# Keeping both parts of every expert unit for the second half of outputs, running the second products one pair later, and decoding weights down to six free slots

## The chip, the core and the metric

The kernel runs on one core of a Trainium2 chip. The metric is the device time of one execution in microseconds, taken over several timed runs; lower is better. The kernel is one program of some 6,600 instructions on five engines: TensorE (PE: matmuls, PEld: loads of the stationary operand), VectorE (DVE), ScalarE (ACT), GpSimd (POOL) and SyncE (SP, which issues every DMA).

## The reference

Two batches of 12 attention heads (448 positions, head size 64) with a tanh cap on the scores, then two feed-forward layers on the 896 x 768 result. Cut to what matters:

```python
scores = cap * np.tanh(q @ k.T / 8 / cap)
attn = softmax(scores);  x = attn @ v                       # (896, 768)
h = x @ w_in                                                # (896, 2048)
P = a[0] + a[1]*h + a[2]*h*h + a[3]*h*h*h
Q = 1.0 + abs(b[0])*abs(h) + abs(b[1])*h*h
g = P / (Q + 1e-6)
x2 = g @ w_out                                              # (896, 768)
y = maximum(maximum(x2 @ w1, x2 @ w2), x2 @ w3)             # (896, 768)
out = y @ w_out2
```

The weights of both layers arrive as 64-bit floats. The result is 32-bit.

## The kernel before, in words

**Numbers.** A matmul operand is held in two parts, a rounded high part and the remainder (`hi`, `lo`), and a product is three matmuls: hi x hi, hi x lo, lo x hi (`three`, line 419). So x, g, x2 and each weight tile exist as pairs of tiles.

**Stages.** Attention comes first: for each of 12 pairs of heads, `prep` loads q, k, v and makes the parts; `scores` (lines 508 to 551) runs the score matmuls (line 520), tanh (L532) and exp (L535); `weighted` (line 553) multiplies with v (L576); the result is copied out of PSUM (`xu`, L588), its row sums travel through DRAM (`sums`, `comp`, `rsum`, `row`), and the scaled result is split into `x{batch}_{pair}` (L630 to L639). Next the first feed-forward layer, in 32 units of 128 hidden channels x 448 tokens, two units to a pair k = 0 to 15. `up` (line 648) makes h of a unit with 18 matmuls (L661). ACT and DVE turn h into g: `A` (L678), `W` (L681, L692, L695), `T` (L685, L687, L700), and for a whole pair `rational` (L716 to L726). `parts` (line 735) splits g of the pair into `gh` (L740) and `gl` (L743). `down` (line 752) multiplies the parts with the weights of the first half of outputs (`oa`) or of the second half (`ob`), nine matmuls a unit (L769). After both halves come the three branches (L851) and the last product (L910).

**Order of the first layer** (lines 797 to 828). Units are made `LAG` = 2 pairs ahead: for each k the program has the parts of k, `up` of pair k+2, then `down("oa")` of pair k. The second half of outputs follows: first the last `KEEP` = 4 pairs, whose parts are still there, then pairs 0 to 11, for which `parts` is called a second time (line 823).

**Weights.** `weight` (line 360) loads a tile in 64 bits into one of three raw buffers and decodes it in six steps: scale (L369 on ACT or L371 on POOL), shift (L375, DVE), rest (L394 on DVE or L391 on ACT), sign (L384, DVE), the high part (L411) and the low part (L399, DVE or POOL).

**What sets the order.** All steps are handed to a planner (`Flow`, line 65) with a cost on each engine that may do them, and it lays them out in time before the program is written; each engine then runs its instructions in exactly that order. A step is due when the PE step that needs it starts; ready steps are taken in order of their due times. SBUF is cut into 52 slots (`NSLOT`); a step that wants a new slot early, more than 14 of the planner's microseconds before it is due, must leave `LEAVE` = 9 of them free (line 123). PSUM is four tiles b0 to b3 of two banks each. In the first layer's first half six banks hold sums (three output blocks x two batches) and two hold the h of the units in work. Waits between engines come with the recorded order: the row lists show that a matmul into one bank of a tile waits for earlier reads of the other bank of that tile.

Of the kernel before, what the change touches and what calls it, by code (L numbers as in the profile page):

```python
# [25 lines left out]
NFC = DFF // P  # L26
# [3 lines left out]
QGUARD = 1.0 + 1e-6  # L30
CAP = 6
NG = 4
LAG = 2
NSLOT, NRAW, NROW = 52, 3, 3
WARM = 4

SPLIT = ()

KEEP = 4

AHEAD, NEAR, LEAVE = 120.0, 24.0, 9

SHARE = 0.5

# [224 lines left out]
def attention_moe(ctx: ExitStack, tc: tile.TileContext, qk, v, w_in, w_out, w123, w_out2, par, out):  # L269
    nc = tc.nc  # L270
    dve, act, pool, pe = nc.vector, nc.scalar, nc.gpsimd, nc.tensor
# [88 lines left out]
    def weight(key, src):  # L360
# [44 lines left out]
        fetched[0] = got  # L405
        s1 = add({"act": 0.80, "pool": 0.87}, scale, [got], [raw, dec], leave=LEAVE, ahead=AHEAD)
        s2 = add({"dve": 0.47}, shift, [s1], [dec], shared=True)
        s3 = add({"dve": 0.87, "act": 0.98}, rest, [s2], [raw, dec], shared=True)
        s4 = add({"dve": 0.87}, sign, [s3], [raw, dec], shared=True)
        s5 = add(  # L410
            {"act": 0.74, "dve": 0.47}, lambda e: copy_on[e](flat(hi), flat(dec)), [s4], [dec, hi],  # L411
# [12 lines left out]
    units += [(fc, b) for fc in range(NG, NFC) for b in range(B)]  # L424
    NU = len(units)
    NK = NU // 2
    again = list(range(NK - KEEP, NK)) + list(range(NK - KEEP))
    for n in range(NG):
        weight(("in", n), w_in[n])
        if n % 2:  # L430
# [1 line left out]
    for j in range(NG // 2, NFC // 2):  # L432
        weight(("in", 2 * j), w_in[2 * j])
        weight(("in", 2 * j + 1), w_in[2 * j + 1])
        weight(("oa", j), w_out[0, j])
    for k in again:
        for fc in dict.fromkeys(units[2 * k + i][0] // 2 for i in range(2)):
            if ("ob", fc) not in weights:
                weight(("ob", fc), w_out[1, fc])
    for oc in range(NCC):  # L440
        for m in range(3):
            weight(("m", oc, m), w123[oc, m])
# [65 lines left out]
    def scores(pi, half):  # L508
# [12 lines left out]

        for t in ts:
            t.early = pi < B * NPAIR - 3
        done = add({"pe": 1.25}, products, prepared, [uq, uk, *ts])
        for th in last_tanh[-2:]:
            th.before(done)
        for j in range(2):
# [25 lines left out]
    def weighted(i):  # L553
# [5 lines left out]
        for half in range(2):  # L559
            x, ex, h = E.pop((i, half))  # L560

            def products(e, half=half, x=x, h=h):
                dst, t = bank(o)[:, :S], two(x)[:CP]
                terms = []
                if h is None:
                    w = flat(vr).rearrange("p (c b d) -> p c (b d)", c=NCH, b=3)
                    for n in range(2):
                        terms.append((w[:CP, 2 * half + n, j * D : j * D + 2 * D], t[:, n]))
                else:
                    w = flat(vs).rearrange("p (t c b d) -> p t c (b d)", t=2, c=2, b=3)  # L570
                    for n in range(2):
                        hi, lo = (w[:CP, z, n, j * D : j * D + 2 * D] for z in range(2))
                        th, tl = two(h)[:CP, n], t[:, n]
                        terms += [(hi, th), (lo, th), (hi, tl)]
                for m, (w_, t_) in enumerate(terms):
                    pe.matmul(dst, w_, t_, start=half == 0 and m == 0, stop=half == 1 and m == len(terms) - 1)  # L576

            dep = add(
                {"pe": 1.66 if h is None else 1.2}, products, [ex, got_v, vl, dep],
                [o, x, vr] + ([h, vs] if h is not None else []),  # L580
            )
            if half == 0 and len(last_copy) > 1:
                last_copy[-2].before(dep)
# [151 lines left out]
    def parts(k):  # L735
        g, dep = G[k]
        hi, lo = slot(f"gh{k}", F32R), slot(f"gl{k}", F32R)

        def high(e):
            copy_on[e](two(hi), two(g))  # L740

        def low(e):
            engine[e].tensor_tensor(out=two(lo), in0=two(g), in1=f32(two(hi)), op=ALU.subtract)  # L743

        h_ = add({"act": 0.845, "dve": 0.54}, high, [dep], [g, hi], shared=True)
        l_ = add({"dve": 1.0, "pool": 2.1}, low, [h_], [g, hi, lo], shared=True)
        GH[k], GL[k] = (hi, h_), (lo, l_)
        G[k] = g, l_

    acc, count = {}, {}  # L750

# [66 lines left out]
    for b in range(B):  # L818
        for o in range(3):
            finish_x2(b, o)  # L820
    for k in again:
        if k < NK - KEEP:
            parts(k)
        down("ob", 2 * k, 1)
        down("ob", 2 * k + 1, 1)
    for b in range(B):
# [152 lines left out]
```

## Time and profile before

| | us |
|---|---|
| median of 3 runs (567.91 to 569.79) | 568.99 |
| the profiled execution | 566.61 |
| its span, first to last instruction | 564.8 |
| PE busy | 536.9 (95%) |
| DVE busy | 402.0 (71%) |
| ACT busy | 318.3 (56%) |
| POOL busy | 58.5 (10%) |

The profile was taken on one execution; the span is the time from its first to its last instruction, and 1.8 us of the execution's time lie around it. Busy shares are means over stages with different limits, so the stages are read one by one. PE's matmuls overlap each other in the records (a matmul of 448 columns is shown with about 365 ns, while the next starts some 200 ns later), so a busy PE is not a proof that nothing holds it, but an idle PE is time lost.

### The profile page before, as it was taken

Reading aid. Unit: us, or ns where it says so; the run is one execution under the profiler, and the core shown is the slowest. Engines: PE = TensorE matmul, PEld = TensorE weight load, DVE = VectorE, ACT = ScalarE, POOL = GpSimd, SP = SyncE. Lnnn points to the kernel's source line nnn. Section 1 sums busy time; section 2 is a strip of 40 time slices with the busy share of each in tenths; the row PEclk is TensorE's granted clock in tenths of the full one; section 3 lists DMA queues with packets and bytes.
Section 4 is the critical chain, followed back from the end, with each engine's and each line's share of the span. In section 5 each row is a group of like instructions: output and inputs, shape, how many; then the busy total and the mean of one; then the engine's idle time right before and its main releaser. Section 6 shows DMA issues by size and latency. Waiting matters only on the chain.

```text
span 564.8 us, 6604 instructions
## 1 busy us (share of the span) xinstructions
PE 536.9 (95%) x2544; PEld 445.2 (79%) x2544; DVE 402.0 (71%) x556; ACT 318.3 (56%) x397; POOL 58.5 (10%) x49
## 2 busy tenths in 40 slices
PE   8999999979978998999899799999999999999997
PEld 5555555548867887887788689999999999999997
DVE  5688999487879999988799989779997473121000
ACT  5899999875567686657776763125443252011111
POOL 0201001100111123010001131210010000000000
PEclk9999999999999999999999899999999999999999
DMA  8666847134000122000132256454455110000112
GB/s 273 220 218 206 274 141 241 63 102 146 18 1 1 56 89 79 2 0 14 43 113 82 86 169 224 167 174 161 169 182 208 57 57 1 1 1 0 57 58 82
DMA packets 17168, 59.79 MB, mean 106 GB/s; under 512 B 3736, under 2 KB 7064, under 8 KB 17136
## 3 DMA queue, kind: packets, MB, share of 16 engines
q1 hardware_dynamic: 17136, 59.36, 30.6%
q8 instruction: 20, 0.33, 0.2%
q14 instruction: 12, 0.10, 0.1%
HBM read 56.47 MB, written 2.88 MB: 105 GB/s over the span
## 4 chain that ended last, share of the span: by engine, by line
PE 66%; DVE 17%; ACT 11%; issue 3%; DMA 3%; SPq 0%; ACTq 0%; DVEq 0%
PE b L851 23%; PE b L769 15%; PE b L661 10%; PE b L910 8%; PE b L576 6%; PE b L520 4%; DMA qk<-in_qk_dram 3%; ACT raw L391 3%; DVE W L723 2%; ACT e L532 2%; DVE W L692 2%; DVE gl L743 2%; DVE W L695 2%; ACT e L535 2%; DVE T L720 2%
## 5 line engine op out<-in xcount | busy, mean ns | idle before, releaser
L851 PE MATMUL b<-x,whm 128*128 128x448 f32 x432 | 122.6, 365 | 0.0
L661 PE MATMUL b<-x,whin 128*128 128x448 f32 x384 | 111.5, 372 | 1.6 <-DVE W L692 1.2
L851 PEld LDWEIGHTS b<-x,whm 128*128 128x128 f32 x432 | 81.1, 188 | 6.4
L576 PE MATMUL b<-e,vr 112*128 112x448 f32 x192 | 80.0, 556 | 2.2 <-issue 2.1
L661 PEld LDWEIGHTS b<-x,whin 128*128 128x128 f32 x384 | 71.8, 188 | 11.3 <-DVE W L692 1.9
L851 PE MATMUL b<-x,wlm 128*128 128x448 f32 x216 | 78.9, 365 | 0.0
L661 PE MATMUL b<-x,wlin 128*128 128x448 f32 x192 | 70.2, 366 | 0.0
L576 PEld LDWEIGHTS b<-e,vr 112*128 112x128 f32 x192 | 34.8, 191 | 36.1 <-issue 31.5
L769 PE MATMUL b<-gh,whoa 128*128 128x448 f32 x96 | 37.3, 389 | 15.6 <-DVE W L692 7.9
L535 ACT ACTIVATE e<-e,con 112x896 f32<-112x896 f32 x48 | 47.9, 1064 | 0.0
L391 ACT ACTIVATE raw<-raw 128x768 uint8<-128x768 uint8 x24 | 46.7, 1956 | 0.1
L532 ACT ACTIVATE e<-b 112x896 f32<-112x896 f32 x48 | 42.3, 944 | 6.9 <-PE b L520 6.9
L851 PEld LDWEIGHTS b<-x,wlm 128*128 128x128 f32 x216 | 40.6, 188 | 3.2
L520 PEld LDWEIGHTS b<-uq,uk 64*112 64x112 f32 x288 | 25.5, 181 | 20.4 <-issue 7.2
L520 PE MATMUL b<-uq,uk 64*112 64x448 f32 x288 | 39.2, 397 | 1.1 <-ACT e L532 1.0
L661 PEld LDWEIGHTS b<-x,wlin 128*128 128x128 f32 x192 | 36.1, 188 | 2.9
L769 PE MATMUL b<-gl,whoa 128*128 128x448 f32 x96 | 36.0, 375 | 2.2 <-DVE gl L743 2.2
L769 PEld LDWEIGHTS b<-gh,whoa 128*128 128x128 f32 x96 | 18.4, 192 | 22.9 <-DVE W L692 10.9
L411 ACT CAST whm<-decm 128x768 fp32r<-128x768 f32 x15 | 12.6, 837 | 42.0 <-DVE decm L384 42.0
L879 ACT CAST h3h<-t 128x448 fp32r<-128x448 f32 x10 | 5.7, 568 | 53.9 <-DVE t L874 53.9
L769 PE MATMUL b<-gh,wloa 128*128 128x448 f32 x96 | 35.7, 372 | 0.0
L769 PE MATMUL b<-gh,whob 128*128 128x448 f32 x96 | 35.2, 366 | 0.3 <-ACT x L785 0.3
(110 smaller groups left out, 976.2 us busy)
## 6 DMA issues: line engine op xcount, KB each, us to landing
raw<-in_w_out_dram SPq DMA_DIRECT2D x22, 768.0 KB, 4.3
raw<-in_w_dram SPq DMA_DIRECT2D x18, 768.0 KB, 4.1
raw<-in_w_in_dram SPq DMA_DIRECT2D x16, 768.0 KB, 5.8
qk<-in_qk_dram SPq DMA_DIRECT2D x12, 448.0 KB, 6.3
vr<-in_v_dram SPq DMA_DIRECT2D x12, 336.0 KB, 4.4
row<-rsum SPq DMA_DIRECT2D x24, 112.0 KB, 3.0
out_dram<-ob SPq DMA_DIRECT2D x6, 384.0 KB, 2.7
out_dram<-ob SPq DMA_DIRECT2D x2, 192.0 KB, 1.9
```

The source lines that it names most:

```text
L391: act.activation(byte[:, 4::8], byte[:, 3::8], AF.Copy, scale=1 / 32, bias=-31 / 64)
L411: {"act": 0.74, "dve": 0.47}, lambda e: copy_on[e](flat(hi), flat(dec)), [s4], [dec, hi],
L520: pe.matmul(pair(ts[j])[:CP, n, :S], k[r, kk, ck], q[r, qq, :], start=m == 0, stop=m == 2)
L532: act.activation(two(x)[:CP], pair(t)[:CP, :, :S], AF.Tanh)
L535: act.activation(two(x)[:CP], two(x)[:CP], AF.Exp, scale=cap[:CP])
L576: pe.matmul(dst, w_, t_, start=half == 0 and m == 0, stop=half == 1 and m == len(terms) - 1)
L661: pe.matmul(bank(h)[:, :S], w_, x_, start=cc == 0 and i == 0, stop=cc == NCC - 1 and i == len(terms) - 1)
L692: dve.tensor_tensor(out=two(w_)[:, i], in0=bank(h)[:, :S], in1=two(w_)[:, i], op=ALU.mult)
L695: dve.scalar_tensor_tensor(out=two(w_)[:, i], in0=two(w_)[:, i], scalar=a1, in1=bank(h)[:, :S], op0=ALU.add, op1=ALU.mult)
L769: pe.matmul(bank(a)[:, :S], w_, g_, start=count[half, o, b] == 1, stop=count[half, o, b] == 3 * NFC)
L851: pe.matmul(bank(o)[:, :S], w_, x_, start=cc == 0 and i == 0, stop=cc == NCC - 1 and i == 2)
L910: pe.matmul(bank(o)[:, :NH], h_, w_, start=i == 0, stop=i == len(terms) - 1)
```

## The change

Five things are edited. `KEEP` and `again` go: the second half of outputs runs over k = 0 to 15 in order and takes the parts that were made for the first half; no part is made twice, and g of a pair gives its slot back after `parts`, while `gh` and `gl` of all 16 pairs stay in 32 slots. The `ob` weights are fetched in the order 0 to 7. `LAG` is 3. `LEAVE` is 6. Three costs that the planner reckons with are other numbers: rest on ACT 1.6, scores 1.5, weighted 1.52 (and 1.25 for a form that isn't used here).

```diff
-LAG = 2
+LAG = 3
-KEEP = 4
-
-AHEAD, NEAR, LEAVE = 120.0, 24.0, 9
+AHEAD, NEAR, LEAVE = 120.0, 24.0, 6
...
-        s3 = add({"dve": 0.87, "act": 0.98}, rest, [s2], [raw, dec], shared=True)
+        s3 = add({"dve": 0.87, "act": 1.6}, rest, [s2], [raw, dec], shared=True)
...
-    again = list(range(NK - KEEP, NK)) + list(range(NK - KEEP))
...
-    for k in again:
-        for fc in dict.fromkeys(units[2 * k + i][0] // 2 for i in range(2)):
-            if ("ob", fc) not in weights:
-                weight(("ob", fc), w_out[1, fc])
+    for j in range(NFC // 2):
+        weight(("ob", j), w_out[1, j])
...
-        done = add({"pe": 1.25}, products, prepared, [uq, uk, *ts])
+        done = add({"pe": 1.5}, products, prepared, [uq, uk, *ts])
...
-                {"pe": 1.66 if h is None else 1.2}, products, [ex, got_v, vl, dep],
+                {"pe": 1.52 if h is None else 1.25}, products, [ex, got_v, vl, dep],
...
-        G[k] = g, l_
...
-    for k in again:
-        if k < NK - KEEP:
-            parts(k)
+    for k in range(NK):
         down("ob", 2 * k, 1)
         down("ob", 2 * k + 1, 1)
```

Because a planner lays out the order, the instructions move on every engine. Three places follow; in the rows of after, line numbers are some six lower (L763 is L769 of before, L656 is L661, L695 is L700, L738 is L743, L397 is L399).

**PE, steady state of the first layer's first half.** Before: the end of `up` of pair 9 (h in tiles b0 and b1) and the `down` of pair 7 behind it.

```order
L661 MATMUL b1_80<-x1_5_1240,wlin9_1074 128x448
L769 MATMUL b2_81<-gh7_1787,whoa3_895 128x448 [waits Activation_49]
L769 MATMUL b2_81<-gl7_1804,whoa3_895 128x448 [waits DVE_49]
...
L769 MATMUL b3_82<-gh7_1787,wloa3_899 128x448
L769 MATMUL b0_79<-gh7_1787,whoa3_895 128x448 [waits DVE_49]
...
L769 MATMUL b0_79<-gh7_1787,wloa3_899 128x448
L769 MATMUL b1_80<-gh7_1787,whoa3_895 128x448 [waits Activation_49]
```

After: the end of `up` of pair 10 (h in b1 and b2) and the `down` of pair 7.

```order
L656 MATMUL b2_81<-x1_5_1238,wlin10_1005 128x448
L763 MATMUL b2_81<-gh7_1741,whoa3_941 128x448
L763 MATMUL b2_81<-gl7_1764,whoa3_941 128x448
...
L763 MATMUL b3_82<-gh7_1741,wloa3_945 128x448
L763 MATMUL b0_79<-gh7_1741,whoa3_941 128x448
...
L763 MATMUL b0_79<-gh7_1741,wloa3_945 128x448
L763 MATMUL b1_80<-gh7_1741,whoa3_941 128x448 [waits DVE_49]
```

Of four waits in the first ten matmuls of a `down` none is left there; one stands at the sixteenth, on the tile of the first unit's h.

**PE, the first units of batch 1.** Before: the `down` of pair 0 (18 matmuls, the last shown here) stands between `up` on `x1_3` and `up` on `x1_4`, `x1_5`.

```order
L661 MATMUL b2_81<-x1_3_1144,wlin2_427 128x448
L769 MATMUL b2_81<-gh0_1211,whoa0_360 128x448 [waits Activation_49]
L769 MATMUL b2_81<-gl0_1220,whoa0_360 128x448 [waits DVE_49]
...
L769 MATMUL b0_79<-gh0_1211,whoa0_360 128x448
L769 MATMUL b0_79<-gl0_1220,whoa0_360 128x448
```

After: no `down` stands there.

```order
L656 MATMUL b2_81<-x1_3_1137,wlin2_429 128x448
L656 MATMUL b1_80<-x1_4_1158,whin0_278 128x448 [waits Activation_49]
L656 MATMUL b1_80<-x1_4_1158,whin0_278 128x448 [waits DVE_49]
L656 MATMUL b1_80<-x1_4_1158,wlin0_287 128x448
L656 MATMUL b1_80<-x1_5_1238,whin0_278 128x448 [waits Activation_49]
```

From the last attention matmul to the first use of `x1_4` PE had 102 matmuls of 448 columns, and now has 84.

**POOL in the same half.** Before: its tensor operations from the second pair on.

```order
L700 TENSOR_TENSOR T2_1287<-T2_1287,A2_1277 128x448 x2
L743 TENSOR_TENSOR gl2_1423<-W2_1273,gh2_1389 128x896
L399 TENSOR_TENSOR wlin10_1510<-decin10_1375,whin10_1481 128x768
L399 TENSOR_TENSOR wlin11_1603<-decin11_1440,whin11_1568 128x768
L743 TENSOR_TENSOR gl4_1697<-W4_1398,gh4_1622 128x896
L399 TENSOR_TENSOR wloa5_1782<-decoa5_1449,whoa5_1735 128x768
L700 TENSOR_TENSOR T9_1863<-T9_1863,A9_1851 128x448 x2
```

After:

```order
L695 TENSOR_TENSOR T2_1287<-T2_1287,A2_1269 128x448 x2
L695 TENSOR_TENSOR T4_1407<-T4_1407,A4_1396 128x448
L695 TENSOR_TENSOR T5_1483<-T5_1483,A5_1468 128x448
L695 TENSOR_TENSOR T6_1571<-T6_1571,A6_1556 128x448
L695 TENSOR_TENSOR T7_1666<-T7_1666,A7_1643 128x448
L397 TENSOR_TENSOR wloa5_1748<-decoa5_1631,whoa5_1734 128x768
L695 TENSOR_TENSOR T9_1834<-T9_1834,A9_1811 128x448
```

Four of the five large operations (low parts of g and of weights) are gone from POOL here; of the small `T` products it has 13 in all, where it had 9.

## Rows read from the trace of the kernel before

**Rows 1.** Windows: stretch, length, busy of PE, PEld, DVE, ACT, POOL, clock, DMA.

```profile
0.00:20.00 20.00, 17.94 (x69) 11.02 (x70) 9.38 (x21) 12.57 (x17) 2.27 (x7) 1.00 0.89 302
20.00:100.00 80.00, 79.53 (x342) 41.69 (x341) 73.25 (x122) 77.43 (x86) 7.76 (x8) 1.00 0.61 202
100.00:133.00 33.00, 29.70 (x117) 17.62 (x116) 21.24 (x36) 25.08 (x28) 1.87 (x2) 1.00 0.30 98
133.00:330.00 197.00, 178.45 (x843) 157.57 (x843) 175.92 (x218) 137.56 (x181) 33.97 (x20) 0.99 0.15 52
```

**Rows 2.** Chain of waits in order of time: start, length, what (matmuls).

```profile
130.88 1.50 PE b L576 x4
...
329.48 56.81 PE b L769 x279
386.29 131.33 PE b L851 x648
```

**Rows 3.** PE's waits, 133 to 330 us: sum, times, longest.

```profile
PE b L769 <- DVE W L692: 7.9, 7, 2.6
PE b L769 <- ACT A L678: 3.1, 3, 1.8
PE b L769 <- DVE gl L743: 2.2, 2, 1.6
PE b L769 <- ACT gh L740: 2.2, 1, 2.2
PE b L769 <- ACT W L681: 2.2, 1, 2.2
```

**Rows 4.** Timeline of PE late in that stretch: start, length, idle before.

```profile
315.94 0.48 PE L769 MATMUL b<-gh,whoa 128*128 128x448 f32 x1 [2.21 <-ACT gh L740]
317.99 0.74 PE L769 MATMUL b<-gl,whoa 128*128 128x448 f32 x1 [1.57 <-DVE gl L743]
318.53 0.57 PE L769 MATMUL b<-gh,wloa 128*128 128x448 f32 x1
...
321.15 0.47 PE L769 MATMUL b<-gh,whoa 128*128 128x448 f32 x1
```

**Rows 5.** DVE by line, 133 to 330 us: count, busy, mean ns, idle before.

```profile
L743 DVE TENSOR_TENSOR gl<-W,gh 128x896 fp32r<-128x896 f32 x26 | 28.5, 1105 | 0.5 <-ACT gh L740 0.5
L723 DVE SCALAR_TENSOR_TENSOR W<-W,con,A 128x896 f32<-128x896 f32 x16 | 24.2, 1511 | 0.0
...
L695 DVE SCALAR_TENSOR_TENSOR W<-W,con,b 128x448 f32<-128x448 f32 x31 | 20.9, 677 | 8.3 <-ACT A L678 4.9 <-PE b L769 3.3
L692 DVE TENSOR_TENSOR W<-b,W 128x448 f32<-128x448 f32 x31 | 19.0, 619 | 8.9 <-ACT A L678 5.3 <-PE b L769 3.3
```

**Rows 6.** Operations on `W`: ns shortest/median/longest, first and last start.

```profile
L743 DVE TENSOR_TENSOR gl<-W,gh x26: 1079/1087/1403, 149.4 to 323.2; 128x896 fp32r<-128x896 f32 x26
...
L723 DVE SCALAR_TENSOR_TENSOR W<-W,con,A x16: 1139/1146/3031, 145.1 to 318.9; 128x896 f32<-128x896 f32 x16
...
L743 POOL TENSOR_TENSOR gl<-W,gh x2: 2657/2814/2972, 174.7 to 211.5; 128x896 fp32r<-128x896 f32 x2
```

**Rows 7.** By line, 0 to 133 us.

```profile
L391 ACT ACTIVATE raw<-raw 128x768 uint8<-128x768 uint8 x9 | 17.5, 1940 | 0.0
...
L588 DVE COPY xu<-b 128x448 f32<-128x448 f32 x21 | 13.0, 621 | 13.1 <-PE b L576 12.9
...
L394 DVE SCALAR_TENSOR_TENSOR decin<-raw,decin 128x768 int32<-128x768 int32 x5 | 5.4, 1071 | 0.1
```

**Rows 8.** Timeline, 144 to 158 us: how the last `x1_5` is made.

```profile
150.39 1.26 DVE L630 TENSOR_TENSOR xu<-xu,row 64x448 f32<-64x448 f32 x2
...
152.01 0.56 ACT L634 CAST x<-xu 128x448 fp32r<-128x448 f32 x1
...
153.82 0.62 DVE L639 TENSOR_TENSOR x<-xu,x 128x448 fp32r<-128x448 f32 x1
```

## The prediction

> **What bounds the kernel now.** I read the stretches first [rows 1]. From 20 to 100 us (attention) PE is busy for 79.5 of 80. From 133 to 330, the first half of the first layer (`up` and `down("oa")`), it is busy for 178.5 of 197: 18.5 us idle. The chain of waits then shows 56.8 us of L769 and 131.3 us of L851 as unbroken pieces of PE [rows 2]: 279 and 648 matmuls, 0.2036 and 0.2027 us each. That is the dense rate, and whatever is edited behind 330 us is hidden under it. At 0.2036 the 843 matmuls of the stretch need 171.6 us, so it loses 25.4: the 18.5 idle, and some 7 in matmuls that come slower.
>
> PE's list of waits tells what the idle time is [rows 3]. Eleven waits (three releasers, 7.9 + 3.1 + 2.2 = 13.2 us) end with DVE or ACT having read an h out of a bank, though the waiting matmul is one of `down`, which reads no h: it writes a sum in the other bank of the same PSUM tile. Three more (2.2 + 2.2 = 4.4 us) end with `gh` or `gl`, parts that were made too late. DVE is the second busiest engine there, 175.9 of 197 [rows 1], and 8.3 + 8.9 = 17.2 us of its 21.1 idle lie before its reads of h, waiting for ACT or PE [rows 5]. PE and DVE wait for each other, which is what more distance between `up` and `down` would loosen.
>
> **The change part by part.** The sum is made against the profiled execution (566.6 us, span 564.8); the median of the runs stands 2.4 us above it, and I move the median by the same difference.
>
> Kept parts. Twelve remakes go, a cast and a subtraction each. They did not lie in the second half, where their products are: all 28 subtractions (26 on DVE, 2 on POOL) start between 149 and 324 us [rows 6], inside the stretch that loses time, since the planner made them early. So they count. By the order, between DVE's first read of an h and its last `gl`, `gl` falls by 10 (10 x 1.105 = 11.1 us [rows 5]), `T` by 4 (near 0.62 each, as the other operation of 448 elements on one tile pair in rows 5: 2.5), and the rest step of decoding rises by 4 (4 x 1.07 = 4.3 [rows 7]); the others nearly cancel. DVE has 9.3 us less to do there: 175.9 becomes 166.6. ACT loses ten casts of `gh`, which its reads of h had to queue behind. Slots are no new shortage: the remade parts were held too, beside the first ones.
>
> Two tiles for h. `down` of a pair had waits at its 1st, 2nd, 7th and 10th matmul; now only the 16th waits. Counted from the end of `up`, the wait for a tile that holds an h comes after 15 x 0.2036 = 3.1 us, where it came after 1.2 or 1.8. The eleven stalls of this kind were 1.2 us in the mean, 2.6 at most; 1.2 to 1.8 us more of cover takes nearly all of each. I leave 1.5 us in total: -11.7. If the cover did nothing, 0; if it did all, -13.2.
>
> One pair more of distance. The parts of a pair get another 54 matmuls of PE work (11 us) before they are needed. The waits for `gh` and `gl` go: -4.4 (bounds -4.4 and, if DVE is late by a whole pair, 0).
>
> What hangs on the waits. The first matmul after an idle time is recorded with 0.47 to 0.48 us instead of 0.36 [rows 4]; at 14 waits that is 1.5 us. After the two waits at 313 to 318 us, 2.21 and 1.57 us of idle PE, the matmuls from 318.53 to 321.15 come every 0.375 us instead of 0.204 and the granted clock of the stretch is 0.99 [rows 1, 4], so PE ran at 1.2 instead of 2.4 GHz there: 8 x 0.17 = 1.4 us. Both should go: -2.9. Together the gains are 11.7 + 4.4 + 2.9 = 19.0.
>
> A new wait. `x1_5`, the last input of batch 1, was ready at 153.82 + 0.62 = 154.4 us, 22.1 us after the last attention matmul ended at 130.88 + 1.50 [rows 2, 8]. Most of that is the trip of the sums through DRAM. PE bridged it with 102 matmuls before the first use of `x1_4`; `down` of pair 0 now comes later, and 84 remain, with 3 on `x1_4`: 87 x 0.2036 = 17.7 us. If the chain takes as long, PE stands for 4.4 us. Its least is some 19.8: the DVE part ran 1.25 us after ACT's cast was done at 152.57, and at least 1.0 us may be won at L630, which had no idle time before it. So 2.1 to 4.4; I take 3.5, nearer to what was seen. Behind this wait on PE stands everything, `down` of pair 0 included, but DVE can work on: +3.5.
>
> Decoding earlier. ACT's price for the rest step sends it to DVE. Before DVE's first read of an h, ACT does 2 of these instead of 8 (6 x 1.94 = 11.6 us less [rows 7]) and DVE 14 instead of 6 (8 x 1.07 = 8.6 us more), and two more weights are decoded there: DVE has some 12 us more to do in the first 130. It had 133 - 103.9 = 29.1 us idle in 0 to 133, 10.6 of these in the first 20 and 11.8 after 100 [rows 1]. Its copies out of PSUM waited for PE for 12.9 us [rows 7], so it was ahead, and 12 us fit into 29, though not with certainty: copies that come late hold the banks of `weighted`. From 0 to +5 us on PE; I take +1.5.
>
> DVE as limit. In the stretch DVE now needs 166.6 and PE 171.6 plus the new 3.5. If DVE's 17.2 us of waits stay, it needs 183.8; PE's length by the terms above is 197 - 19.0 + 3.5 = 181.5. So DVE asks for 2.3 us more than PE, or for nothing if its waits shrink; were its load not to fall at all, 175.9 + 17.2 = 193, 11.6 more. I take +2.
>
> Second half, branches, last product, and the fetching of `ob` in another order: nothing, under dense PE [rows 2]; a weight of this half serves 36 matmuls, 7.3 us.
>
> Sum: -19.0 + 3.5 + 1.5 + 2.0 = -12.0. The profiled execution would be near 554.6 and the median 568.99 - 12.0 = **557.0**.
>
> **Two rules of the Trainium skill.** L723 takes 1.146 us in the median and 3.03 at the longest, while a low part on POOL takes 2.7 to 3.0 [rows 6]. The Trainium skill, page "SBUF — State Buffer", section "Who interferes with whom", says that a DVE instruction with two SBUF inputs contends with a GpSimd instruction that reads SBUF, and that the first to start holds the port to its end. By that rule four large POOL operations fewer would give DVE back up to 4 x 1.9 = 7.5 us, some of it taken again by four more `T`, and DVE would ask for nothing beyond PE: a sum of -14. The sum above goes without it.
>
> PE at half clock followed idle time here [rows 4]. The Trainium skill, page "TensorE: Matmul & The Clock Gate", section "HAM oscillation — how this bites in real kernels", says that idle gaps bring the throttle back. By that rule the new wait, the longest of all, brings one slow piece of its own, 1.4 us at the size seen: a sum of -10.6. The trace has waits of 2.6 and 2.2 us with no such piece behind them.
>
> **Rivals.**
> 1. All stalls of the stretch go, the slower matmuls too, and the chain to `x1_5` takes its least: -25.4 + 2.1, **546 to 549**. For it: DVE's load falls. Against: PE would have to run dense beside a DVE that is busy for 95% of it.
> 2. DVE is the limit and keeps its idle time. What is taken from it behind its first read of an h (9.3) was put ahead of it (12), so its last `gl` falls at the same time or 2.7 us later, and PE with it: **569 to 571.5**. For it: DVE's 89% in the stretch [rows 1]. Against: 17.2 of its 21.1 us of idle are waits for PE and ACT [rows 5], which end when other work is ready. To the same time leads a change that doesn't do what it says: the eleven stalls only move from the 7th and 10th matmul to the 16th, 13.2 us stay, and 4.4 and a part of the 2.9 stand against 3.5 and 1.5: 567 to 569.
> 3. Slower: the trip of the sums. DVE is the limit as in rival 2, and at the new wait before `x1_4` and `x1_5` it runs out of work too, since the reads of h that would come next wait for the PE that waits. Then DVE's idle time grows by the new wait, 2.1 to 4.4, and by the copies that come late in attention, up to 5, on top of the 2.7: **572 to 580**. It decides as soon as DVE's idle time up to its last `gl`, 29.1 + 21.1 = 50.2 us now, passes 51. For it: the order takes 18 matmuls of cover away just there. Against: by the order DVE has the decoding of two weights and the g of pairs 0 and 1 to do in that place.
>
> **How the numbers follow.** A difference of 0.3% (1.7 us) is about what a measurement of this kernel can tell from none. Forecast 0.62, its own range 551 to 563 (a new wait of 2.1 to 4.4, attention 0 to 5, DVE 0 to 4). Rival 1: 0.13. Rival 2: 0.14, of which 0.03 faster, 0.07 the same, 0.04 slower. Rival 3: 0.11. Faster: 0.62 + 0.13 + 0.03 = 0.78; the same 0.07; slower 0.15. From 548 to 568 lie the forecast, half of rival 1 and the lower part of 2: 0.8 with little to spare.
>
> **What would show it.** Right: PE's waits at L763 (L769 of before) fall from 17.6 us to under 4; a wait of 2 to 4.5 us appears on L656 before `x1_4` or `x1_5`; no slow clock near the end of the first half; POOL without `gl`; the pieces behind the first half unchanged within 0.5 us. Wrong: as much idle at L763 with DVE above 95% (rival 2); DVE and PE idle together before `x1_4` and DVE late ever after (rival 3); PE idle on L571 in attention for more than 5 us; waits for an `ob` weight after the first half.

## The result, and the profile after

The changed kernel takes 554.1 us (median of four runs, 551.8 to 555.21), the kernel before 568.45 on the same chip (four runs, 567.24 to 569.79): a ratio of 0.9742, 95% interval 0.9699 to 0.9785, or 14.35 us less. 557.0 was forecast, with 548 to 568 as the range. The profiled execution took 555.21 us, its span is 553.3 (564.8 before). Executions that took over 1.5% longer than the fastest of their kernel are left out of the medians and ratios below.

The stretches of the changed kernel (columns as in [rows 1]; the first layer's first half now ends near 318.5):

```profile
0.00:20.00 20.00, 17.17 (x76) 10.51 (x77) 10.90 (x25) 14.34 (x20) 1.71 (x7) 1.00 0.83 262
20.00:100.00 80.00, 76.05 (x322) 39.62 (x321) 72.00 (x115) 70.86 (x84) 7.25 (x7) 0.98 0.67 212
100.00:133.00 33.00, 32.05 (x131) 18.86 (x130) 30.57 (x50) 23.47 (x28) 0.92 (x1) 1.00 0.47 150
133.00:318.50 185.50, 179.91 (x869) 163.32 (x868) 164.01 (x213) 121.67 (x165) 23.89 (x17) 0.99 0.15 50
```

PE is idle for 5.6 us of the last stretch, where it was idle for 18.5. DVE has 11.9 us less to do there, POOL is busy for 23.9 us, where it was for 34.0. The second row shows a loss: from 20 to 100 us PE was idle for 4 us (0.5 before) and ran a part at a lower clock; from 100 to 133 us it was idle for 1.0 instead of 3.3.

What PE waited for from 133 to 318.5 us, against [rows 3]:

```profile
PE b L763 <- ACT W L676: 2.5, 1, 2.5
PE b L763 <- DVE W L687: 1.4, 2, 0.7
PE b L656 <- DVE x L634: 0.6, 1, 0.6
PE b L763 <- ACT x L779: 0.6, 1, 0.6
PE b L656 <- DVE W L690: 0.3, 1, 0.3
```

The 17.6 us of [rows 3] are 3.9 now (2.5 + 1.4); no wait for a part of g is left. The three waits stand at the first matmul of the `down` of pair 0, the 7th of pair 1 and the first of pair 13.

The end of attention, and the last pieces of the chain of waits (start, length, what), against [rows 2]:

```profile
130.73 1.67 PE L571 MATMUL b<-e,vr 112*128 112x448 f32 x4
```

```profile
314.58 53.18 PE b L763 x261
...
370.20 41.19 PE b L843 x198
...
430.47 74.67 PE b L843 x360
...
505.85 43.97 PE b L902 x252
```

That gives the account of the 11.5 us between the two spans. (The medians lie 14.35 apart: the execution profiled before was 2.4 us faster than the median given with it, the one profiled after 1.1 us slower than its own. "Half clock" below comes back to this.) Attention ends at 132.40 (132.38 before): 0. From there to the first branch matmul it takes 237.8 us (253.9): -16.1. The branches take 505.85 - 370.20 = 135.65 (131.33): +4.3. The last product: +0.3. The second term is the change; the third is looked at in e8, whose profiled execution had a span of 550.7.

DVE's costliest groups from 133 to 318.5, against [rows 5] and the L723 of [rows 6]:

```profile
L690 DVE SCALAR_TENSOR_TENSOR W<-W,con,b 128x448 f32<-128x448 f32 x31 | 20.6, 675 | 1.6 <-PE b L763 1.4
L687 DVE TENSOR_TENSOR W<-b,W 128x448 f32<-128x448 f32 x31 | 19.2, 621 | 7.1 <-ACT A L673 4.7 <-ACT W L676 1.3 <-PE b L763 0.7
L715 DVE SCALAR_TENSOR_TENSOR T<-T,qone,A 128x896 f32<-128x896 f32 x16 | 18.4, 1147 | 7.4 <-ACT A L712 7.4
L718 DVE SCALAR_TENSOR_TENSOR W<-W,con,A 128x896 f32<-128x896 f32 x16 | 18.3, 1145 | 0.0
L738 DVE TENSOR_TENSOR gl<-W,gh 128x896 fp32r<-128x896 f32 x16 | 17.5, 1094 | 2.0 <-ACT gh L735 2.0
```

Ten `gl` are gone (28.5 to 17.5 us), as forecast. Not forecast: L718, sixteen times before and after, fell from 24.2 to 18.3 us, 1511 to 1145 ns each. Its neighbour L715 fell too:

```profile
L720 DVE SCALAR_TENSOR_TENSOR T<-T,qone,A 128x896 f32<-128x896 f32 x16 | 21.6, 1353 | 1.1 <-issue 1.0
```

is the row of the kernel before. Together 9.1 us, with not one instruction removed. e12 is about these.

### The profile page after: what moved, and what is told of

Its sections match the earlier page's. It is cut to its first block, busy times and chain, and to the rows that moved or that the text cites. A ratio compares the mean times of both kernels' runs of the same rounds, so it can differ in the third digit from the quotient of the medians.

```text
span 553.3 us, 6572 instructions
## 1 busy us (share of the span) xinstructions
PE 535.2 (97%) x2544; PEld 444.3 (80%) x2544; DVE 398.1 (72%) x562; ACT 287.3 (52%) x373; POOL 44.7 (8%) x43
## 4 chain that ended last, share of the span: by engine, by line
PE 76%; DVE 13%; ACT 6%; issue 2%; DMA 2%; SPq 0%; ACTq 0%; DVEq 0%
PE b L843 22%; PE b L763 18%; PE b L656 16%; PE b L571 9%; PE b L902 8%; PE b L515 3%; DVE xu L625 1%; ACT W L676 1%; DVE W L687 1%; ACT raw L389 1%; DMA row<-rsum 1%; ACT e L527 1%; ACT A L673 1%; ACT e L530 1%; DVE decin L382 1%
## 5 line engine op out<-in xcount | busy, mean ns | idle before, releaser
L843 PE MATMUL b<-x,whm 128*128 128x448 f32 x432 | 124.5, 369 | 0.2 <-DVE t L861 0.2
L656 PE MATMUL b<-x,whin 128*128 128x448 f32 x384 | 111.3, 371 | 1.4 <-DVE x L634 0.6
L656 PEld LDWEIGHTS b<-x,whin 128*128 128x128 f32 x384 | 71.9, 188 | 10.2 <-issue 1.3
L656 PE MATMUL b<-x,wlin 128*128 128x448 f32 x192 | 70.3, 366 | 0.0
L763 PE MATMUL b<-gh,whoa 128*128 128x448 f32 x96 | 36.3, 378 | 4.1 <-ACT W L676 2.5
L515 PEld LDWEIGHTS b<-uq,uk 64*112 64x112 f32 x288 | 23.8, 171 | 19.4 <-issue 9.8
L656 PEld LDWEIGHTS b<-x,wlin 128*128 128x128 f32 x192 | 36.2, 189 | 2.8
L676 ACT ACTIVATE W<-b,con 128x448 f32<-128x448 f32 x32 | 23.0, 723 | 28.8 <-PE b L656 25.2
L515 PE MATMUL b<-uq,uk 64*112 64x448 f32 x288 | 36.1, 378 | 1.2 <-ACT e L527 0.8
L763 PE MATMUL b<-gh,whob 128*128 128x448 f32 x96 | 35.3, 368 | 0.9 <-ACT x L779 0.9
L763 PE MATMUL b<-gl,whoa 128*128 128x448 f32 x96 | 35.5, 370 | 0.0
L763 PE MATMUL b<-gh,wloa 128*128 128x448 f32 x96 | 35.5, 370 | 0.0
L763 PE MATMUL b<-gh,wlob 128*128 128x448 f32 x96 | 35.1, 365 | 0.0
L763 PE MATMUL b<-gl,whob 128*128 128x448 f32 x96 | 35.1, 365 | 0.0
L409 ACT CAST whm<-decm 128x768 fp32r<-128x768 f32 x14 | 11.7, 837 | 38.2 <-DVE decm L382 38.2
```

The lines of the kernel that those rows point to most:

```text
L515: pe.matmul(pair(ts[j])[:CP, n, :S], k[r, kk, ck], q[r, qq, :], start=m == 0, stop=m == 2)
L656: pe.matmul(bank(h)[:, :S], w_, x_, start=cc == 0 and i == 0, stop=cc == NCC - 1 and i == len(terms) - 1)
L676: act.activation(two(w_)[:, i], bank(h)[:, :S], AF.Identity, bias=a2, scale=a3)
L763: pe.matmul(bank(a)[:, :S], w_, g_, start=count[half, o, b] == 1, stop=count[half, o, b] == 3 * NFC)
L843: pe.matmul(bank(o)[:, :S], w_, x_, start=cc == 0 and i == 0, stop=cc == NCC - 1 and i == 2)
```

## The experiments

Every time below is a median with its ratio to the kernel before on the same chip. The kernel before took 567.04 us beside e1 to e4, 567.96 beside e5 to e8, 568.72 beside e9 to e11 and 567.53 beside e12. "The stretch" is the time from the last attention matmul to the first branch matmul, by the ends and starts of single matmuls, which lie 0.2 us from the pieces of the chain: 253.7 us before, 237.6 in the changed kernel, 239.6 in its second profile (e8).

### Which part pays: kept parts or distance

**e1, the parts of all pairs kept, nothing else.**

```
-KEEP = 4
+KEEP = 16
```

> The kernel before with the parts of all 16 pairs made once and kept, and the second half in the order 0 to 15; distance 2, nine free slots, old costs. In the steady state `down` still waits at its 7th and 10th matmul for the tiles of h. Theory D (distance): the stalls of PE go because `down` waits later and its parts are a pair older; this kernel has neither, so 564 to 568 us, 0 to 4 us under before, and PE's idle time before `down` of the first half stays above 11 of 17.6 us. Theory L (load): the stalls go because DVE has ten `gl` less to make there; 557 to 560 us, idle time under 8.

556.62 us, ratio 0.9819 (0.9775 to 0.9863): 10.4 us faster. PE meets the tiles of PSUM in the same order as in the kernel before, with a sum and an h in one tile at the same matmuls of a `down`, and yet the waits shrink; the time lies just under theory L's range. PE's waits from 133 to 320 us:

```profile
PE b L769 <- DVE gl L743: 4.0, 2, 3.3
PE b L769 <- ACT A L678: 1.8, 1, 1.8
PE b L769 <- DVE W L692: 1.4, 2, 0.7
```

W L692 is down from 7.9 us in 7 waits to 1.4 in 2, A L678 from 3.1 to 1.8, with no distance added. In all 8.1 us are left at `down` of 17.6, half of them late `gl` near the end; the stretch took 244.9. DVE is busy for 160.6 of these 187 us, 15.3 less than before: 10.8 in the ten `gl` and 6.7 in L723 and L720, whose number is the same (see e12); other steps rose by 2. But e1 takes work from ACT too, twelve casts of `gh`, and two `gl` from POOL. How much of the gain is DVE's and how much ACT's, no run here separates.

**e2, three pairs of distance, nothing else.**

```
-LAG = 2
+LAG = 3
```

> The kernel before with a distance of 3 pairs and nothing else; `down` waits at its 16th matmul for a tile of h, parts are still made twice. Theory D: 555 to 559 us, PE's idle time before `down` of the first half under 7 us. Theory L: 563 to 567 us, since DVE's load before 330 us is that of before; idle time above 11 us, DVE busy for over 93% of the stretch.

565.92 us, ratio 0.9949 (0.9912 to 0.9987): 2.9 us by the ratio, 1.1 by the medians. The order of tiles is that of the changed kernel, with waits of `down` at its 7th matmul in pairs 1 to 3 and at its 16th from pair 4 on, and yet much of the waits stays. From 131 to 325 us:

```profile
PE b L769 <- ACT A L678: 3.6, 2, 3.3
PE b L769 <- DVE W L695: 2.6, 3, 1.3
PE b L769 <- ACT gh L740: 2.3, 1, 2.3
PE b L769 <- ACT W L681: 1.9, 1, 1.9
```

With 0.8 us for `gl` these are 11.2 us of 17.6, so they fell by a third. It matters where they stand. From pair 4 on, the waits for reads of h are 2.1 us, where they were 6.6 before (1.7 in e1): there the order does what was said of it. But 6.1 us stand in pairs 0 to 2 and 3.1 at parts that are late in pair 15, in spite of the added pair. Nor does the stretch get shorter: it took 253.8 in this execution (253.7 before), at a granted clock of 0.96, and DVE is busy for 169.0 of 194, 87%, where theory L had over 93%. So distance alone brings little time; less work brings most of it.

**e3, the whole change but for the distance.**

```
-LAG = 3
+LAG = 2
```

(against the changed kernel)

> The changed kernel with a distance of 2 pairs: parts kept, six free slots, new costs. `down` waits at its 7th and 10th matmul again. Theory D: 562 to 567 us, idle time before `down` above 10 us. Theory L: 555 to 559 us, idle time under 7 us.

566.72 us, ratio 0.9988 (0.9946 to 1.0029). The stretch is 10 us shorter (243.4), so the gain of e1 is there; it is given back before it begins, since the last attention matmul ends at 143.1. PE's waits from 20 to 143 us:

```profile
PE b L571 <- DVE xu L583: 6.4, 4, 2.7
PE b L656 <- DVE W L690: 1.9, 1, 1.9
```

and the granted clock is 0.96 there:

```profile
20.00:100.00 80.00, 72.95 (x296) 37.63 (x296) 65.31 (x103) 64.40 (x75) 11.30 (x9) 0.96 0.63 197
100.00:143.00 43.00, 39.64 (x159) 22.91 (x156) 34.93 (x55) 31.36 (x38) 3.47 (x2) 0.96 0.48 147
```

This is the mechanism of "decoding earlier": DVE decodes weights, its copies of `xu` out of PSUM are late, and the matmuls that want those banks wait. Priced at 0 to 5 us, it cost 10.7 in this order. Why so much, is not shown: sixteen weights are decoded here before attention ends, but so they are in e6 and e9, with fewer rest steps on DVE (12 and 9 instead of 14), and there attention ends at 129.9 and 132.3; the changed kernel has the same 14 and ends it at 132.4.

### Where h lies in PSUM

**e4, the two h of the units in work pinned to one tile, the sums to the other three.**

```
+            pin = {"h": (0, 1), "acc": range(2, 8)}.get(v.kind if v.name[0] == "h" or v.name.startswith("acc0") else None, range(8))
-            order = [(4,), (5,)] if v.kind == "av" else [(i,) for i in range(8)]
+            order = [(4,), (5,)] if v.kind == "av" else [(i,) for i in pin]
```

> The kernel before, with both banks that hold the h of units put into one PSUM tile (banks 0 and 1) and the six sums into the other three, so that no sum shares a tile with an h; distance, parts, slots and costs as before. If the 13.2 us of `down` waiting for reads of h come from the shared tile, they go: at most 1 us is left of them before `down`, and what is left stands before `up`, which needs the bank itself 18 matmuls (3.7 us) later. Theory D: 556 to 561 us. Theory L: DVE is the limit and the wait only moves from `down` to `up`: 565 to 569 us with as much idle time in the stretch.

600.99 us, ratio 1.0609 (1.0553 to 1.0664). `down` then waits for no h, as meant, but `up` of one unit waits for the reads of the other unit's h at most units, four rows with 36.5 us in sum. The first (the profiled execution took 609.81 us):

```profile
PE b L662 <- DVE W L696: 25.8, 15, 3.5
```

Both theories missed this; the wait takes the place of the one removed (13.2 us) and is longer.

**e9, the parts kept and LEAVE 6, two pairs, old costs.**

```
-KEEP = 4
+KEEP = 16
...
-AHEAD, NEAR, LEAVE = 120.0, 24.0, 9
+AHEAD, NEAR, LEAVE = 120.0, 24.0, 6
```

> The kernel before with the parts of all sixteen pairs kept and LEAVE 6; second products two pairs later and the planner's three costs as they were. With the costs of the change too (LAG 2) attention ended at 143.1 us and the whole took 568.8; without LEAVE 6 and without the costs it was 556.6 with attention to 132.7. Theory P (LEAVE pays for the slots that the longer way holds, so at two pairs it has nothing to pay for; the long attention came from weights that are decoded earlier, that is from LEAVE): last attention product 138 to 145, stretch behind it 242 to 245 us, 562 to 570 us in all. Theory C (the long attention came from the planner's costs): last attention product 130 to 134, stretch 239 to 243 us, 551 to 556 us.

579.33 us, ratio 1.0166 (1.0108 to 1.0223): neither theory. Attention ended at 132.3, so LEAVE alone does not lengthen it; the stretch took 263.0. By the order, the planner put both h of a pair into one tile (b1) for the whole half, e4 by accident, and the trace shows e4's waits:

```profile
PE b L661 <- DVE W L695: 18.9, 11, 3.2
PE b L769 <- DVE gl L743: 2.3, 2, 1.3
PE b L661 <- DVE W L692: 2.3, 2, 1.1
```

So how far a wait for h can be hidden depends on the tiles that the planner happens to choose: e1 has 0.7 us of such waits at L661 in place of 21.8, and is some 20 us faster (0.9819 against 1.0166).

### Do the parts add up

**e5, kept parts and three pairs; LEAVE 9 and old costs.**

```
-LAG = 2
+LAG = 3
...
-KEEP = 4
+KEEP = 16
```

> The kernel before with two of the changes together: the parts of all sixteen pairs kept, and the second products three pairs later; LEAVE stays 9 and the planner's three costs stay as they were. One after another, the two gave 10.3 us and 2.9 us of the 14.4. Theory S (the two add up, and the costs and LEAVE are worth nothing): 553 to 556 us, last attention product near 132, first half of outputs and second half of the first layer together 238 to 241 us (253.7 before, 237.6 in the changed kernel), waits at the first layer's products under 6 us in all. Theory I (the distance pays only together with the costs and LEAVE): 557 to 561 us, that stretch 243 us or more, the waits at the matmuls for the sums of h back, 8 us or more of lost time there.

562.51 us, ratio 0.9915 (0.9887 to 0.9942): just above theory I's range, and slower than e1, which had two pairs. Stretch 247.8, last attention matmul 134.9.

**e6, the changed kernel with the old costs.**

```
-        s3 = add({"dve": 0.87, "act": 1.6}, rest, [s2], [raw, dec], shared=True)
+        s3 = add({"dve": 0.87, "act": 0.98}, rest, [s2], [raw, dec], shared=True)
...
-        done = add({"pe": 1.5}, products, prepared, [uq, uk, *ts])
+        done = add({"pe": 1.25}, products, prepared, [uq, uk, *ts])
...
-                {"pe": 1.52 if h is None else 1.25}, products, [ex, got_v, vl, dep],
+                {"pe": 1.66 if h is None else 1.2}, products, [ex, got_v, vl, dep],
```

> The changed kernel with the planner's three old costs (0.98 for ScalarE's part of a weight's rest, 1.25 for score products, 1.66 and 1.2 for value products); everything kept, three pairs, LEAVE 6. Theory S: within 1.5 us of the changed kernel, 552.5 to 555.5 us, since the costs only say where a step is put. Theory I: the weights' rest steps move to ScalarE in attention and more of VectorE's late copies turn into waits at the score products: last attention product 135 to 140 instead of 132.4, and 557 to 562 us.

555.31 us, ratio 0.9771 (0.9739 to 0.9802); its interval overlaps that of the changed kernel beside it (e8). The costs are worth 2.4 us by the medians, which the intervals cannot tell from nothing; theory S had 1.5 at most, theory I over 4. Since e6 is e5 with LEAVE 6, LEAVE is worth 7 us at three pairs.

**e7, the changed kernel with LEAVE 9.**

```
-AHEAD, NEAR, LEAVE = 120.0, 24.0, 6
+AHEAD, NEAR, LEAVE = 120.0, 24.0, 9
```

> The changed kernel with LEAVE at 9 instead of 6 (weights decoded while more than nine slots are free, instead of six); everything else as changed. Theory S: 552.5 to 555.5 us, attention the same within 1 us. Theory I: fewer weights are decoded ahead, so the waits at the first layer's products for weights and for the sums of h come later in the unit and cost more: the stretch behind attention 240 to 243 us instead of 237.6, 556 to 559 us in all.

560.72 us, ratio 0.9882 (0.984 to 0.9923), stretch 243.5: theory I's kind, a little beyond its range. LEAVE, to which the prediction gave no gain, is worth 7 to 8 us at three pairs, more than the distance by itself.

**e8, the changed kernel once more.**

> The changed kernel itself once more, beside the others. Two things are looked at. First the time of a matmul in the branches at the end: 207 ns each in the profiled execution of the changed kernel and 203 ns before; if this belongs to the kernel it is 207 ns again and the stretch of the branches takes 135 us; if it belongs to that execution alone it is 203 ns and 131 to 133 us. Second the two pieces at half clock (43.5 to 46.9 and 159.6 to 163.0 us), each behind a wait of 2.5 us: both are there again if the waits are of the same length. Time 552 to 555 us.

552.96 us, ratio 0.9733 (0.9703 to 0.9764). Pieces of its chain:

```profile
429.25 73.24 PE b L843 x360
503.20 43.99 PE b L902 x252
```

The 360 branch matmuls take 73.24 us, 203.4 ns each; in the first profile they took 74.67, 207.4 ns each. So about 2 of the 4.3 us lost in the branches there belong to that execution. The branches take 133.6 us here (503.20 - 369.62): the other 2 us recur, waits for `t` from DVE (0.7 us before the first matmul of the last product, 0.5 and 0.1 inside) and the slower matmuls behind each. Of the two waits of 2.5 us the one behind the first `up`s is there again (2.52 us) with its half clock; the one in attention is 1.1 us now and has none, and attention ends at 129.9. The stretch took 239.6.

### Further along the same two numbers

**e10, the changed kernel with LEAVE 3.**

```
-AHEAD, NEAR, LEAVE = 120.0, 24.0, 6
+AHEAD, NEAR, LEAVE = 120.0, 24.0, 3
```

> The changed kernel with LEAVE 3: weights are decoded while more than three slots are free. From nine to six it gave about 7 us (560.7 to 553 to 554), with one weight more decoded before the end of attention (15 instead of 14). Theory M (more room, more gain): 16 or 17 weights decoded before attention ends, stretch behind it 233 to 238 us, 549 to 552.5 us. Theory E (six is enough; what is decoded earlier makes VectorE's copies in attention late): last attention product 133 to 140, stretch within 2 us of the changed kernel's 237.6 to 239.6, 553 to 562 us.

560.18 us, ratio 0.9844 (0.9775 to 0.9913): theory E. Sixteen weights are decoded before attention ends at 135.6, and PE waits 6.4 us for `xu`, as in e3.

**e11, the changed kernel at four pairs.**

```
-LAG = 3
+LAG = 4
```

> The changed kernel with the second products four pairs of units later instead of three. Theory D (distance is what takes the waits away): the 4.3 us that are still lost at the matmuls for the sums of h go to under 2, 550 to 553 us. Theory P (each pair more holds slots, and what was free for weights decides): waits for weights or for free slots come back, stretch behind attention 241 to 246 us, 555 to 562 us, as three pairs did with LEAVE 9 (243.5 us, 560.7).

562.27 us, ratio 0.9872 (0.98 to 0.9943), stretch 249.8: theory P's side, beyond both its ranges. The waits that come back are not for weights or slots, though, but for W (L687 4.4 us, L690 3.9 at L763): DVE is late again.

### What GpSimd costs VectorE

In the kernel before, DVE's two longest L723 stand beside two low parts on POOL. DVE, then POOL (start, length):

```profile
199.91 2.74 DVE L723 SCALAR_TENSOR_TENSOR W<-W,con,A 128x896 f32<-128x896 f32 x1
...
212.43 3.03 DVE L723 SCALAR_TENSOR_TENSOR W<-W,con,A 128x896 f32<-128x896 f32 x1
```

```profile
198.93 2.77 POOL L399 TENSOR_TENSOR wlin<-decin,whin 128x768 fp32r<-128x768 f32 x1 [9.91 <-ACT whin L411]
211.53 2.97 POOL L743 TENSOR_TENSOR gl<-W,gh 128x896 fp32r<-128x896 f32 x1 [9.83 <-DVE wlin L399]
```

POOL's subtraction ends at 211.53 + 2.97 = 214.50 and DVE's operation, begun meanwhile, at 215.46, 0.96 later; alone it takes 1.14. It stood nearly all the time that POOL ran. Over all groups, the DVE operations of the stretch that exceed the median of their line by more than 0.6 us were 7 in the kernel before and lost 9.9 us; in the changed kernel 2 and 1.7 us (e8: 4 and 2.9). Each of them overlaps an operation on POOL.

**e12, sixteen more subtractions on POOL** (gh - gl of each pair into the tile of g, behind `gl`; nobody reads it).

```
+        def extra(e):
+            engine[e].tensor_tensor(out=two(g), in0=f32(two(hi)), in1=f32(two(lo)), op=ALU.subtract)
+        add({"pool": 0.05}, extra, [l_], [g, hi, lo], due=fl.clock + 2.0)
```

> The changed kernel with one more GpSimd subtraction for each of the sixteen pairs (gh - gl of a pair into the tile of g, read by nobody, behind gl), 896 elements, near 2.1 to 2.8 us each by the same operation of the kernel before; the planner is told that it costs 0.05, so that the rest stays nearly where it is (the matmuls meet the tiles of PSUM in the same order). In the stretch between attention and the branches VectorE operations that took over 0.6 us more than the median of their kind lost 9.9 us in all in the kernel before, 1.7 to 2.9 in the changed one, 7.9 with LEAVE 9 and old costs, 10.1 with LEAVE 3 and 10.5 at four pairs, each beside GpSimd's subtractions. Theory K (the collision of the two engines is part of what the kernels lose): lost 8 us or more in such operations, waits of PE on W up by 4 us or more, 557 to 564 us. Theory N (VectorE has room, GpSimd beside it is free): 552.5 to 556 us, the lengthened operations notwithstanding.

578.93 us, ratio 1.0171 (1.0106 to 1.0236), where e8 had 0.9733: the mechanism of theory K, at some 25 us far beyond its range. The first layer's first half (columns as in [rows 1]), and the groups of POOL and of DVE in it:

```profile
136.00:340.00 204.00, 182.58 (x841) 162.65 (x840) 178.41 (x205) 114.67 (x155) 72.30 (x35) 0.96 0.11 38
```

```profile
L744 POOL TENSOR_TENSOR W<-gh,gl 128x896 f32<-128x896 f32 x16 | 45.8, 2866 | 63.9 <-DVE gl L738 63.8
```

```profile
L718 DVE SCALAR_TENSOR_TENSOR W<-W,con,A 128x896 f32<-128x896 f32 x16 | 23.9, 1494 | 0.0
L715 DVE SCALAR_TENSOR_TENSOR T<-T,qone,A 128x896 f32<-128x896 f32 x16 | 21.6, 1353 | 11.9 <-ACT A L712 11.9
```

L718 and L715 are back at 1494 and 1353 ns, the kernel before's 1511 and 1353. Nineteen DVE operations between attention and the branches are lengthened, by 26.2 us. PE's waits at `down` for W follow: 12.0 us for DVE (7.9 + 4.1) and 3.8 for ACT. A second path is in the trace too: ACT waits 5.0 us, in two waits, for a `T` that POOL makes, where it had no such wait in the changed kernel; what each path costs is not separated. The planner moved a few of the other steps as well, so the price of one collision is not read from the total, but from the rows: DVE is held for what is left of POOL's operation.

## Why the prediction was right

The mechanism held: PE and DVE waited for each other in the first layer's first half, and the change loosened it; -14.35 us against -12.0. That the sum came so near is in part luck. Between the two profiled executions the stretch became 16.1 us shorter, where its terms come to 13.5 (-19.0 + 3.5 + 2.0); attention kept its length, where +1.5 stood; and 4.6 us were lost in the branches and the last product, where nothing stood. These misses cancel to -11.5. Step by step:

**Stalls on tiles of h, late parts, restarts (-19.0 in sum).** The waits fell from 17.6 to 3.9 us, under the 4 that were named. But the step gave all of the 11.7 to one part of the change: "1.2 to 1.8 us more of cover" from another order of tiles. e2 has that cover and keeps 11.2 us of the waits (-2.9 us in all); e1 lacks it and keeps 8.1 (-10.4). From pair 4 on, either edit alone takes most of the waits for reads of h (6.6 us before, 2.1 in e2, 1.7 in e1); in the early pairs and for late parts distance alone fell short. The -4.4 for `gh` and `gl` was given to the added pair, and e2, which has it, still waits 3.1 us for them.

**DVE's load and "DVE as limit" (+2).** DVE is busy 164.0 us in the stretch, 166.6 was forecast, and its ten `gl` fell by 11.0 (11.1 forecast). The total is near by luck: of the 11.9 us that DVE lost, 9.1 are those of L715 and L718, which the sum left out, so the operations that were counted came to 2.8 and not to 9.3. Six rest steps were added (5.9 us) and not four, and DVE took over low parts of weights from POOL (7.1 to 9.5 us). The 9.1 us that L715 and L718 had lost to POOL stood in the sentences on the Trainium skill alone, page "SBUF — State Buffer", section "Who interferes with whom": a DVE instruction with two inputs in SBUF and a GpSimd instruction that reads SBUF exclude each other, and the one that starts first keeps the other out. These rows agree (212.43 to 215.46 beside 211.53 to 214.50), and e12 brings it back. By that rule the sum was -14; the runs gave -14.35, a nearness that owes as much to the misses above. With PE's waits down to 3.9 us, DVE asked for nothing beyond PE: the +2 was too high by 2.

**The new wait before x1_4 and x1_5 (+3.5, least 2.1).** It is there, but 0.6 us long. `x1_5` was ready 18.8 us after the last attention matmul, not 22.1, below the least of 19.8 that the step allowed:

```profile
140.40 0.22 DVE L603 TENSOR_SCALAR comp<-comp,guard 64x14 f32<-64x14 f32 x1
150.57 0.62 DVE L634 TENSOR_TENSOR x<-xu,x 128x448 fp32r<-128x448 f32 x1
```

(132.40 to 151.19). The least let only two late steps of the chain shrink; most was won earlier. In both kernels the sums are back from DRAM at 139.1 to 139.3 us. The changed kernel takes them up 1.1 us later (L603), the kernel before 3.5 us later, behind other work of DVE and a wait of 0.9 us for ACT:

```profile
142.67 0.22 DVE L608 TENSOR_SCALAR comp<-comp,guard 64x14 f32<-64x14 f32 x1
```

That is 2.3 us of the 3.3; the rest was won behind it.

**Attention (+1.5).** A miss in both directions. Two waits for late `xu` appeared (3.6 us, 2.5 the longest, and a piece at half clock behind it), but two of 2.1 and 1.2 at its end went, and the last matmul ends where it did (0), or 2.5 us earlier in e8. What the term could become is seen in e3 (+10.7) and in e10.

**LEAVE.** No gain was given to decoding with less room left. e7 against e8 and e5 against e6 show 7 to 8 us at three pairs; e9 and e10 show that it can be lost again. One weight more is decoded before attention ends (15 instead of 14). What goes with the time are the DVE operations lengthened beside POOL: among the kernels that keep the parts they cost 9.4 us in e5, 5.6 in e7, 9.2 in e10 and 10.5 in e11, all over 560 us, and 1.7 to 4.0 in the changed kernel, e1 and e6, all under 557. e5 and e6 differ in LEAVE alone, and put the sums and the h into nearly the same tiles; by these rows up to 5.4 of the 7.2 us between them (9.4 against 4.0) may be such collisions. No run tests this for LEAVE, and e3 and e9 are slow without them (3.6 and 1.5 us). Why LEAVE makes 7 us is not settled: the planner lays out another order for each number, and a part of what each of e3, e5, e7, e9, e10 and e11 shows may be the luck of that order. What is shown: with the parts kept, three pairs were faster than two only with LEAVE 6 (e1 and e5, e3 and e8), and LEAVE 6 was faster than 9 only at three pairs (e1 and e9, e5 and e6). The cause is open.

**Half clock.** The Trainium skill, page "TensorE: Matmul & The Clock Gate", section "HAM oscillation — how this bites in real kernels", was read as one slow piece behind the new wait. There is none behind that wait (0.6 us) and two behind others, of 2.51 us in attention and 2.53 us. Behind the second PE runs for nine matmuls at 1.2 GHz, one each 0.37 us:

```profile
158.09 0.47 PE L763 MATMUL b<-gh,whoa 128*128 128x448 f32 x1 [2.53 <-ACT W L676]
...
160.38 0.57 PE L763 MATMUL b<-gh,whoa 128*128 128x448 f32 x1
160.75 0.57 PE L763 MATMUL b<-gl,whoa 128*128 128x448 f32 x1
161.13 0.57 PE L763 MATMUL b<-gh,wloa 128*128 128x448 f32 x1
```

That piece costs nine times 0.17, about 1.5 us; the first, eight products in 4.97 us that take 3.24 elsewhere, 1.7. [rows 4] had one such piece, now there are two, so of the 2.9 only restarts were won between these two executions. Over more executions it is otherwise. The mean granted clock was 0.984 to 0.996, 0.990 in the mean, in the 46 executions of the kernel before that were timed beside the experiments, and 0.993 to 0.997, 0.996 in the mean, in the eight of the changed kernel. The one of the kernel before that was profiled had 0.996, so [rows 4] shows less of the half clock than that kernel usually has. An estimate from these numbers: a mean clock lower by 0.006 over 566 us is 2 x 0.006 x 566 = 7 us more at 1.2 GHz, and half of that is lost time. So some 3 us of the 14.35 may be clock, about what the medians show more than the profiled executions; among the 46 the time follows the clock only loosely, so it may be less.

**Second half, branches, last product (0).** The second half runs as before, 0.2038 us a matmul (53.18 / 261; 0.2036 before), and the last product is 0.3 us longer; the branches lost 2.3 us in e8 to waits for DVE that the kernel before has not, which no step foresaw. Why DVE comes late there is not shown.

**The rivals.** Rival 1 (546 to 549) failed by the waits left in attention and before the first `down`, and by the branches. Rival 2, waits that stay with DVE as limit, did not come: DVE is busy for 88% of the stretch and the waits are gone; e2 (565.9) comes near to its time, with DVE at 87%. Rival 3 needed DVE to be late in attention; e3 shows that part, and it ends even with the kernel before instead of slower because the stretch still gains. No run beat the changed kernel; e6 and e1 come next.

## What to carry to other kernels

When PE waits for a bank and DVE waits for PE, look first at what can be taken off DVE, and only then at more distance between producer and consumer: here less load gave 10.4 us alone and the distance 2.9. Compare the mean of a group with its median: where the mean stands well above (1511 against 1146 ns), look what another engine does beside the long ones; here it was POOL, and with less work there the time came back without an edit of the instruction. Take a clock from several executions and not from the profiled one alone. Where a planner sets the order, an edit of one number must be measured in each combination it will run in, since its parts do not add up (e1 556.6, e5 562.5, e9 579.3).

## What was not expected of the hardware

The branch matmuls came every 207.4 ns in one execution and every 203.4 in another of the same kernel, evenly over 360 matmuls and at a granted clock of 1.00. Other traces have both spacings: 207 in the branches of e6, e7 and e9, and in e10 207 turns into 203 inside the branches, behind a wait of 0.58 us. In e8 it is 207 from about 160 to 250 us; some 430 matmuls at 4 ns are most of the 2 us by which its stretch is longer than in the first profile. The cause is open. A wait of PE of the same length is followed by half clock in one place and not in another: 2.51, 2.53 and 2.52 us (changed kernel, e8) with it, 2.54 (e7) and 2.59 us (kernel before) without. And POOL's subtraction pays for a collision too. In e12 the sixteen took 2.13 to 5.66 us; DVE ran nothing when the first of these two began; while the second ran, DVE made six operations, four of them with two inputs in SBUF, and the next (L715) then took 3.02 us:

```profile
156.08 2.13 POOL L744 TENSOR_TENSOR W<-gh,gl 128x896 f32<-128x896 f32 x1 [5.50 <-DVE gl L738]
...
225.16 5.66 POOL L744 TENSOR_TENSOR W<-gh,gl 128x896 f32<-128x896 f32 x1 [7.63 <-DVE gl L738]
```
